# Additions of the drains in the later quarters: VectorE, two per unit over four units, in place of GpSimd, four per unit over two

## The chip, the cores and the metric

The kernel runs on one core of a Trainium2 chip. The metric is the device time of one execution in microseconds. The kernel before took 713.81 us in the median of three runs (713.41 to 713.83). The engines are named as in the profile: PE is TensorE, DVE is VectorE, ACT is ScalarE, POOL is GpSimd, SP is the engine whose queue issues the DMAs.

## The reference

A layer of an FNet block and then a gated feed-forward layer, on x of 2048 rows by 448 columns in float32. Cut to what matters:

```
def _A_ref(x, ...):                          # Fourier mixing, real part only
    a = einsum("bsd,ed->bse", x, dft_hid_re)
    b = einsum("bsd,ed->bse", x, dft_hid_im)
    return einsum("ts,bse->bte", dft_seq_re, a) - einsum("ts,bse->bte", dft_seq_im, b)

def _B_ref(x, w_gate, w_up, w_down):         # 448 -> 1792 -> 448
    g = einsum("bsd,df->bsf", x, w_gate)
    u = einsum("bsd,df->bsf", x, w_up)
    return einsum("bsf,fd->bsd", gelu(g) * u, w_down)

h = x + _A_ref(layernorm(x), ...)
h2 = h + _B_ref(layernorm(h), w_gate, w_up, w_down)
```

The change touches only the very end of the last line: the sum of h and the down projection.

## The kernel before

The Fourier layer fills about the first 346 us. After it the feed-forward layer runs in 42 units, numbered t = 0 to 41, of one gate-and-up step each (`GateUp`): 14 for the first half of the rows, 14 for a third quarter of them, 14 for the fourth. From unit 14 on a unit also carries one or two steps d of the down projection (`COUNT`), 42 in all; the last 14 of 56 steps follow after unit 41.

The matrix products are done by a scheme of seven products in place of eight (Strassen's), and each operand is split into a high and a low half in float16. Every product is made of three matmuls: high by high, high by low and low by high.

**The down projection.** The output is made in eight pieces p = 0 to 7 of 256 rows, here called quarters as the change's title does; seven steps d make one. A step d goes through these stages, each on its engine:

- `hid_load(d)`: SP loads hid[d] (256 KB) from the memory where the gate-and-up units left it.
- `dn_sums(d)`: DVE makes the five sums dn_s of the scheme, three instructions (lines 1174 to 1176).
- `dn_hi(d)`: ACT rounds hid and dn_s to the high halves, in dn_w (line 108).
- `dn_lo(d)`: DVE subtracts these and writes the low halves, in dn_w (line 112). Some steps, done early, write to other places (hops, dn_l, dn_xs).
- `dn_mm(d)`: PE does 21 matmuls into four banks acc_d (line 1212); the third of a step is the first to read a low half.

In unit t the loads and sums are for the steps of unit t + 2, the halves for those of unit t + 1.

**The drain.** When the seven steps of a quarter p are over, at the end of unit t0 (18, 23, 27, 32 and 37 for p = 0 to 4), `Drain` takes the banks to the output piece hr[p], which holds h. ACT copies banks 0 and 1 into v0 and v1 (line 940). DVE adds banks 2 and 3 to hr straight from there (line 944). Then eight additions or subtractions of 128 x 224 in float32, `sums`, bring the four products in v0 and v1 to the four parts of hr (line 972); two read v0, two v1, two v0, two v1. The tiles v0 and v1 exist once: the next quarter's copies must wait for the readers of the last. At last `dn_store(p)` writes hr[p] out (line 1230).

**What sets the order.** It is written out by hand: each engine works through its instructions in the order in which the code issues them, and waits by semaphores for the others. The end of a unit's code is, in this order: the copies and bank additions when a quarter ends, the last gelu (line 1102 on ACT, then a product on POOL, line 1104), the remaining low halves, the sums `dn_sums`, and last the loop over the ended quarters, which the change edits. The next unit's first instruction on DVE is line 1089 (`y3`), which waits for PE; then line 1020 twice (`z2`, `y2`), then the low halves. On SP the next unit's first is `gw_load` (896 KB of weights), which waits for PE, then `hid_load`.

Before the change POOL's eight additions come at the ends of units t0+1 and t0+2, four each, and the store at the end of t0+3.

Of the kernel before, what the change touches and what calls it, by code (L numbers as in the profile page):

```python
# [32 lines left out]
def kernel(  # L33
# [40 lines left out]
    V, A, G, PE = nc.vector, nc.scalar, nc.gpsimd, nc.tensor  # L74
# [242 lines left out]
    class Weights:  # L317
# [8 lines left out]
        def sums(self):  # L326
            gate, up = self.raw[:, 0], self.raw[:, 1]
            s = self.s = prep.tile([P, 10, P], F32, tag="s", name=f"gu_s{self.f}")
            V.tensor_add(s[:, 0:3], up[:, 0:3], up[:, 3:6])
            V.tensor_sub(s[:, 3:6], s[:, 0:3], gate[:, 0:3])  # L330
            V.tensor_sub(s[:, 6:8], gate[:, 0:2], up[:, 0:2])
            V.tensor_sub(s[:, 8:10], gate[:, 4:6], s[:, 4:6])
# [87 lines left out]
    def step_of(n):  # L420

        k, qq = divmod(n - NT, 4)
        return 2 + k // 2, k % 2, qq
# [392 lines left out]
    for n in range(N_STEPS):  # L816
# [78 lines left out]
        else:  # L895
            p, part, qq = step_of(n)
# [29 lines left out]
    class Drain:  # L926
# [27 lines left out]
        def bank3(self):  # L954
            self.add(3, 6, 1.0)

        def sums(self, parts):
            x11, x12, x21, x22 = self.x
            M3, M4, M2, M5 = self.v
            ops = (  # L960
                (G.tensor_add, x12, M3),
                (G.tensor_sub, x21, M4),
                (G.tensor_add, x21, M2),
                (G.tensor_add, x12, M5),
                (G.tensor_sub, x11, M4),
                (G.tensor_add, x22, M3),
                (G.tensor_sub, x11, M5),
                (G.tensor_sub, x22, M2),
            )
            for k in parts:  # L970
                op, x, m = ops[k]
                op(x, x, m)  # L972
# [143 lines left out]
    def gw_load(t):  # L1116
        gw[t] = w_tile(f"gw{t}")
        nc.sync.dma_start(gw[t], w_dram[f_of(t)])
# [4 lines left out]
    def hid_load(d):  # L1123
        p, n = divmod(d, NC)
        hid_in[d] = fpool.tile([P, 4, P], F32, tag="hid", bufs=6, name=f"hid{d}")
        b = max(p // 2 - 1, 0)
        nc.sync.dma_start(hid_in[d], hid_dram[b, n][:, p % 2 if b else p])
# [32 lines left out]
    def dn_sums(d):  # L1160
        t = dn_hid(d)
        if d in LAST:
            spare.append(d)
            s = fops.tile([P, 5, P], F32, tag=("xn", "tt")[len(spare) % 2], name=f"dn_s{d}")
        elif d % 4 < 2:
            if d % 4 == 0:
                opened["l"] = late.tile([P, 10, P], F32, tag="dn_s", name=f"dn_s{d}")
            s = opened["l"][:, d % 4 * 5 :][:, :5]
        else:
            if d % 4 == 2:  # L1170
                opened["s"] = prep.tile([P, 10, P], F32, tag="s", name=f"dn_s{d}")
            s = opened["s"][:, d % 4 % 2 * 5 :][:, :5]
        dn_s[d] = s
        V.tensor_add(s[:, 0:2], t[:, 0:2], t[:, 2:4])  # L1174
        V.tensor_sub(s[:, 2:4], t[:, 1:4:2], t[:, 0:4:2])  # L1175
        V.tensor_add(s[:, 4], t[:, 0], t[:, 3])  # L1176
# [4 lines left out]
    def dn_hi(d):  # L1181
        dn_w[d] = dn_tile(d)
        for src, dst in dn_parts(d):
            hi_part(dn_w[d][:, 0, dst], src)

    def dn_lo(d):
        for src, dst in dn_parts(d):
            lo_part(dn_w[d][:, 1, dst], src, dn_w[d][:, 0, dst])
# [13 lines left out]
    def dn_mm(d, products=range(21)):  # L1202
        p, n = divmod(d, NC)
        if n == 0 and 0 in products:
            dn_banks(p)
        w = dn_w[d]
        for i in products:
            k, m = divmod(i, 3)
            a, b = STRASSEN[k]
            la, lb = ((0, 0), (0, 1), (1, 0))[m]  # L1210
            ps, opens = acc_d[p, "sums"][k]
            PE.matmul(  # L1212
                ps,
                w[:, la, a, :],
                wd[n][:, lb, b, :],
                start=n == 0 and m == 0 and opens,
                stop=n == NC - 1 and m == 2,
                skip_group_check=True,
            )

    def hr_load(p):
        hr[p] = pair_tile(f"hr{p}")
        nc.sync.dma_start(hr[p], h_dram[p])

    def dn_drain(p):
        v = [fpool.tile([P, D], F32, tag=f"v{k}", bufs=1, name=f"v{k}_{p}") for k in range(2)]
        return Drain(hr[p], acc_d.pop(p), v, 1.0 / (H_SC * W_SC))

    def dn_store(p):
        nc.sync.dma_start(outr[p // 4, p % 4], hr[p])  # L1230
# [4 lines left out]
    def do(t, k):  # L1235
        for what in side.pop((t, k), ()):
            what()
# [41 lines left out]
    for t in range(NF):  # L1279
        w = gu.get(t + 2) if t + 2 in JIT_F else None  # L1280
        n = PREP_AT.get(t)
# [89 lines left out]
    drains, ended = {}, {}  # L1371
    for t in range(NF, N_GU):
        now, ahead = steps[t], steps.get(t + 1, [])
        split = EARLY.get(t - 1)
        if t + 2 < N_GU:
            gw_load(t + 2)
        far = steps.get(t + 2, []) + ([EARLY[t + 1]] if t + 1 in EARLY else [])
        far += [47] if t + 1 == N_GU else []
        for d in far + ([52, 53, 54] if t + 1 == N_GU else []):
            hid_load(d)  # L1380
        for d in ahead:
            if d % NC == 0:
                hr_load(d // NC)
        if t in (N_GU - 4, N_GU - 2):
            hr_load(6 + (t == N_GU - 2))
        dn_mm(now[0], range(0, 6))
        prev.y3()
        if t % 2 == 0:
            prev.store()
        cur.y1()  # L1390
        if now[0] % NC:
            cur.z1()
        cur.x2()
        dn_mm(now[0], range(6, 13 if len(now) == 1 else 21))
        for d in ahead:
            dn_hi(d)
        if split is not None:
            dn_hi(split)
        cur.z2()
        do(t, 1)  # L1400
        cur.y2()
        for d in ahead[:1]:
            dn_lo(d)
        if len(now) == 1:
            dn_mm(now[0], range(13, 21))
        else:
            dn_mm(now[1])
        ends = now[-1] % NC == NC - 1
        ends = ends and t + 1 < N_GU
        if ends:  # L1410
            p = now[-1] // NC
            ended[p], drains[p] = t, dn_drain(p)
            drains[p].copy((0,))
        prev = cur
        if t + 1 < N_GU:
            cur = GateUp(t + 1)
            cur.x1()
        if ends:
            drains[p].copy((1,))
            drains[p].bank2()  # L1420
            drains[p].bank3()
            cur.z1()
        prev.c_last()
        for d in ahead[1:]:
            dn_lo(d)
        if split is not None and t + 1 < N_GU:
            dn_lo(split)
        for d in far:
            dn_sums(d)
        do(t, 2)  # L1430
        do(t, 3)
        do(t, 4)
        for p, t0 in ended.items():
            if p < 5 and t - t0 in (1, 2):
                n = 4 * (t - t0)
                drains[p].sums(range(n - 4, n))
            if p < 5 and t - t0 == 3:
                dn_store(p)

    prev.y3()  # L1440
# [99 lines left out]
```

## Time and profile before

| what | value |
|---|---|
| median of three runs | 713.81 us |
| profiled execution, its own time | 712.2 us |
| its span, first to last instruction | 710.2 us |
| PE busy, share of the span | 703.0 us, 99% |
| DVE busy | 531.8 us, 75% |
| ACT busy | 353.2 us, 50% |
| POOL busy | 119.6 us, 17% |
| TensorE clock granted | 1.000 |

A row of the timeline has the start in us from the span's start, the duration, the engine, the line, the operation, output<-inputs, the shape and type, how many were merged, and in brackets how long the engine had been idle and what ended it. A row of groups has the count, then the busy time and the mean in ns of one, then the idle time before them. A row of windows has, after the stretch and its length, the busy time and count on PE, PEld, DVE, ACT and POOL, then the granted clock, the share of the DMA engines and GB/s. A row of waits has who waited for whom, the total, the times and the longest.

### The profile page before, as it was taken

What the parts mean: (1) busy time and instruction counts of PE and PEld (TensorE: products, weight loads), DVE (VectorE), ACT (ScalarE), POOL (GpSimd) and SP (SyncE); (2) the same over time, 40 slices, a digit from 0 to 9 for tenths busy, and PEclk for the clock granted to TensorE, in tenths of its full rate; (3) what the DMA queues carried; (4) which work ended last, traced back from release to release, by engine and by line L of the source; (5) the groups of instructions that cost most, each with busy time, mean ns of one, the idle gap of its engine ahead of it and who ended that gap; (6) DMA issues with size and microseconds to landing.
All of it is one profiled execution on the core that took longest, in us unless ns stands there. A gap on an engine that the chain in (4) does not pass through costs nothing.

```text
span 710.2 us, 13038 instructions
## 1 busy us (share of the span) xinstructions
PE 703.0 (99%) x4952; PEld 480.1 (68%) x4952; DVE 531.8 (75%) x1136; ACT 353.2 (50%) x656; POOL 119.6 (17%) x128
## 2 busy tenths in 40 slices
PE   9999999999999999999999999999999999999998
PEld 5555555555555555797744444469999999989897
DVE  7988637486848779998647787567777866799785
ACT  5776523162526454543436566545555453555531
POOL 0000000000000000000223333311141522352624
PEclk9999999999999999999999999999999999999999
DMA  8788539999898969653755867797797986877512
GB/s 272 244 250 262 124 137 232 238 320 246 207 305 237 269 209 223 257 139 112 173 179 191 280 211 199 199 319 245 192 323 256 258 282 231 295 268 272 206 37 79
DMA packets 116031, 159.42 MB, mean 224 GB/s; under 512 B 61952, under 2 KB 80512, under 8 KB 115968
## 3 DMA queue, kind: packets, MB, share of 16 engines
q1 hardware_dynamic: 115968, 158.60, 73.3%
q8 instruction: 38, 0.62, 0.3%
q14 instruction: 25, 0.20, 0.1%
HBM read 110.33 MB, written 34.34 MB: 204 GB/s over the span
## 4 chain that ended last, share of the span: by engine, by line
PE 95%; DVE 3%; DMA 1%; issue 0%; POOL 0%; SPq 0%; DVEq 0%; POOLq 0%
PE acc L648 33%; PE acc_d L1212 14%; PE pY L1010 14%; PE y L714 9%; PE pZ L1010 9%; PE pX L1010 9%; PE acc_f L520 7%; DMA hid<-hid_dram 1%; DVE dn_s L1175 1%; PE pw L102 1%; DVE dn_s L1174 0%; DVE dn_s L1176 0%; DVE dn_w L112 0%; DVE hops L112 0%; DVE hr L1476 0%
## 5 line engine op out<-in xcount | busy, mean ns | idle before, releaser
L648 PE MATMUL acc<-xs,ws 128*128 128x448 f16 x1248 | 238.0, 352 | 0.0
L648 PEld LDWEIGHTS <-ws 128*128 128x128 f16 x1248 | 122.0, 98 | 114.0 <-DVE ws L114 0.2
L1010 PEld LDWEIGHTS <-gw 128*128 128x128 f16 x1365 | 133.4, 98 | 42.9
L1212 PE MATMUL acc_d<-wd,dn_w 128*128 128x224 f16 x1008 | 111.2, 259 | 2.4 <-DVE dn_w L112 2.4
L1212 PEld LDWEIGHTS <-dn_w 128*128 128x128 f16 x1008 | 96.7, 98 | 5.2 <-DVE dn_w L112 3.2
L1104 POOL TENSOR_TENSOR hs<-hs,c 128x256 f32<-128x256 f32 (+1 forms) x42 | 55.3, 1316 | 225.1 <-ACT c L1102 150.3
L1010 PE MATMUL pY<-hops,gw 128*128 128x256 f16 (+1 forms) x595 | 89.9, 294 | 0.0
L114 DVE SCALAR_TENSOR_TENSOR ws<-wr,ws 128x1024 f16<-128x1024 f32 (+2 forms) x66 | 75.1, 1141 | 8.6 <-ACT ws L108 8.3
L108 ACT ACTIVATE ws<-wr 128x1024 f16<-128x1024 f32 (+2 forms) x66 | 63.8, 981 | 21.5 <-DMA wr<-in_w_seq_dram 20.8
L220 POOL TENSOR_TENSOR wd_s<-wd 128x448 f32<-128x448 f32 x7 | 9.4, 1349 | 342.8 <-DVE r_h L142 342.0
L714 PE MATMUL y<-wh,z 128*128 128x448 f16 x336 | 66.2, 352 | 0.0
L1010 PE MATMUL pX<-hops,gw 128*128 128x256 f16 (+1 forms) x385 | 61.7, 294 | 0.0
L1010 PE MATMUL pZ<-hops,gw 128*128 128x256 f16 (+1 forms) x385 | 61.7, 294 | 0.0
L714 PEld LDWEIGHTS <-z 128*128 128x128 f16 x336 | 32.9, 98 | 30.1
L1020 DVE SCALAR_TENSOR_TENSOR c<-pZ,u 128x256 f32<-128x256 f32 (+1 forms) x42 | 21.4, 510 | 37.8 <-PE pZ L1010 22.3
L520 PEld LDWEIGHTS <-ws 128*128 128x128 f16 x504 | 48.3, 98 | 0.9
L1010 PEld LDWEIGHTS <-gu_w 128*128 128x128 f16 x273 | 26.6, 98 | 31.9 <-issue 0.2
L1055 ACT ACTIVATE pY<-pX 128x256 f32<-128x256 f32 (+1 forms) x42 | 18.4, 439 | 59.3 <-PE pX L1010 58.9
L1066 ACT ACTIVATE u<-pY 128x256 f32<-128x256 f32 (+1 forms) x42 | 19.1, 454 | 55.6 <-PE pY L1010 55.5
L972 POOL TENSOR_TENSOR hr<-hr,v 128x224 f32<-128x224 f32 x56 | 41.8, 772 | 14.7 <-ACT v L940 13.8
L108 ACT ACTIVATE dn_w<-dn_s 128x640 f16<-128x640 f32 x48 | 35.0, 729 | 18.0 <-DVE dn_s L1176 18.0
L112 DVE TENSOR_TENSOR dn_w<-dn_s,dn_w 128x640 f16<-128x640 f32 x48 | 41.6, 867 | 2.0 <-ACT dn_w L108 1.9
(138 smaller groups left out, 880.3 us busy)
## 6 DMA issues: line engine op xcount, KB each, us to landing
gw<-w_dram SPq DMA_DIRECT2D x35, 896.0 KB, 5.4
wr<-in_w_seq_dram SPq DMA_DIRECT2D x100, 256.0 KB, 4.5
hid_dram<-hs SPq DMA_DIRECT2D x27, 512.0 KB, 5.9
hid<-hid_dram SPq DMA_DIRECT2D x54, 256.0 KB, 5.6
w_dram<-gu_w SPq DMA_DIRECT2D x14, 896.0 KB, 5.7
gu_raw<-in_w_gu_dram SPq DMA_DIRECT2D x28, 384.0 KB, 5.9
wr<-in_w_seq_dram SPq DMA_DIRECT2D x14, 512.0 KB, 5.2
x<-in_x_dram SPq DMA_DIRECT2D x16, 224.0 KB, 2.8
```

Source lines behind the costliest of these rows:

```text
L108: A.activation(dst, src, AF.Copy, scale=scale)
L112: V.tensor_sub(dst, src, hi)
L114: V.scalar_tensor_tensor(dst, src, scale, hi, op0=ALU.mult, op1=ALU.subtract)
L520: PE.matmul(fast_sum(n, k), fast_a(n, i, lw, a), fast_b(j, lx, b), start=j == 0 and m == 0 and k % 2 == 0, stop=j == NT // 2 - 1 and m == ...
L648: PE.matmul(acc[key][:, :D], w[:, lw, block * P : (block + 1) * P], xs[c][:, lx, :], start=c == 0 and m == 0, stop=c == NT - 1 and m == 2,)
L714: PE.matmul(y[:, :D], z[p][:, lz, k, g * P : (g + 1) * P], wh[:, lw, k, :], start=k == 0 and m == 0, stop=k == 6 and m == 2,)
L972: op(x, x, m)
L1010: PE.matmul(ps, w[:, wl, wa + ws, :], ops[:, m + ms, :], start=first and n == 0, stop=last and n == len(terms) - 1, skip_group_check=True,)
L1020: V.scalar_tensor_tensor(dst, ps, SC, other, op0=ALU.mult, op1=ALU.add)
L1066: A.activation(self.u2, self.Y, AF.Copy, scale=SC)
L1104: G.tensor_mul(c22, c22, self.cols(self.c12))
L1212: PE.matmul(ps, w[:, la, a, :], wd[n][:, lb, b, :], start=n == 0 and m == 0 and opens, stop=n == NC - 1 and m == 2, skip_group_check=True,)
```

## The change

```diff
-        def sums(self, parts):
+        def sums(self, parts, E=G):
             x11, x12, x21, x22 = self.x
             M3, M4, M2, M5 = self.v
             ops = (
-                (G.tensor_add, x12, M3),
-                (G.tensor_sub, x21, M4),
+                (E.tensor_add, x12, M3),
+                (E.tensor_sub, x21, M4),
...
         for p, t0 in ended.items():
-            if p < 5 and t - t0 in (1, 2):
-                n = 4 * (t - t0)
-                drains[p].sums(range(n - 4, n))
-            if p < 5 and t - t0 == 3:
+            n = 2 * (t - t0)
+            if p < 5 and 2 <= n <= 8:
+                drains[p].sums(range(n - 2, n), V)
+            if p < 5 and n == 8:
                 dn_store(p)
```

The other six operations change G to E in the same way. For the quarters p = 0 to 4 the eight additions go to DVE (`V`), two at the ends of units t0+1 to t0+4; the store goes to the end of t0+4. Quarters 5 and 6, after the units, still call `sums(range(8))` and stay on POOL.

What this makes of the engines' orders is shown at three places. Names carry the number of the step, unit or quarter and then one that a builder gives: dn_s32 is the sum of step 32, hr3 and v1_3 are of quarter 3. A name ending in _49 is a semaphore, by the engine or DMA queue that raises it.

First, DVE at the end of unit 34, the stretch ahead of units 35 and 36. Before:

```order
L1174 TENSOR_TENSOR dn_s32_7237<-hid33_7125 128x256 [waits DMAHW2_49]
L1175 TENSOR_TENSOR dn_s32_7237<-hid33_7125 128x256
L1176 TENSOR_TENSOR dn_s32_7237<-hid33_7125 128x128
L1174 TENSOR_TENSOR dn_s50_7244<-hid50_7127 128x256 [waits DMAHW3_49,DVE_49]
L1175 TENSOR_TENSOR dn_s50_7244<-hid50_7127 128x256
L1176 TENSOR_TENSOR dn_s50_7244<-hid50_7127 128x128
L1089 SCALAR_TENSOR_TENSOR hs_34_7193<-pY_34_7096,g1_34_7164 128x2x128 [waits PE_49]
```

The same place now:

```order
L1174 TENSOR_TENSOR dn_s32_7235<-hid33_7123 128x256 [waits DMAHW2_49]
L1175 TENSOR_TENSOR dn_s32_7235<-hid33_7123 128x256
L1176 TENSOR_TENSOR dn_s32_7235<-hid33_7123 128x128
L1174 TENSOR_TENSOR dn_s50_7242<-hid50_7125 128x256 [waits DMAHW3_49,DVE_49]
L1175 TENSOR_TENSOR dn_s50_7242<-hid50_7125 128x256
L1176 TENSOR_TENSOR dn_s50_7242<-hid50_7125 128x128
L972 TENSOR_TENSOR hr3_6341<-hr3_6341,v1_3_6981 128x224 x2
L1089 SCALAR_TENSOR_TENSOR hs_34_7191<-pY_34_7096,g1_34_7162 128x2x128 [waits PE_49]
```

A pair of additions now stands between the sums and y3; the pair has no wait for another engine.

Second, the boundary of units 27 and 28, where quarter 2 ends only four units after quarter 1. ACT before:

```order
L940 ACTIVATE v0_2_6437<-acc_d2_0_6000 128x448 [waits PE_49,Pool_49]
L1055 ACTIVATE pY_28_6441<-pX_28_6440 128x256 [waits DVE_49,PE_49]
L940 ACTIVATE v1_2_6438<-acc_d2_1_6001 128x448 [waits Pool_49]
L1061 ACTIVATE m5_28_6461<-pZ_28_6454 128x256 [waits PE_49,Activation_49]
L1102 ACTIVATE c12_27_6405<-c12_27_6405 128x256 [waits DVE_49]
```

ACT now:

```order
L940 ACTIVATE v0_2_6434<-acc_d2_0_6000 128x448 [waits DVE_49,PE_49]
L1055 ACTIVATE pY_28_6438<-pX_28_6437 128x256 [waits DVE_49,PE_49]
L940 ACTIVATE v1_2_6435<-acc_d2_1_6001 128x448 [waits DVE_49]
L1061 ACTIVATE m5_28_6458<-pZ_28_6451 128x256 [waits PE_49,Activation_49]
L1102 ACTIVATE c12_27_6402<-c12_27_6402 128x256 [waits Pool_49]
```

And DVE now at the end of unit 27, the rows that the second copy waits for:

```order
L944 SCALAR_TENSOR_TENSOR hr2_5882<-acc_d2_3_6003,hr2_5882 128x224 [waits DVE_49,PE_49]
L1174 TENSOR_TENSOR dn_s22_6462<-hid22_6337 128x256 [waits DMAHW6_49]
L1175 TENSOR_TENSOR dn_s22_6462<-hid22_6337 128x256
L1176 TENSOR_TENSOR dn_s22_6462<-hid22_6337 128x128
L1174 TENSOR_TENSOR dn_s22_6462<-hid23_6339 128x256 [waits DMAHW7_49]
L1175 TENSOR_TENSOR dn_s22_6462<-hid23_6339 128x256
L1176 TENSOR_TENSOR dn_s22_6462<-hid23_6339 128x128
L972 TENSOR_TENSOR hr1_5321<-hr1_5321,v1_1_5958 128x224 x2
L1089 SCALAR_TENSOR_TENSOR hs_26_6284<-pY_27_6316,g1_27_6377 128x2x128 [waits PE_49]
```

The copies waited for POOL, whose additions of quarter 1 stand in units 24 and 25; now they wait for DVE, the first copy for the pair at the end of unit 26, the second for the last pair, which the code issues after the copy in the same unit. By the values of the semaphore it is the second of the two L972 rows above.

Third, SP around the store of quarter 3, before:

```order
L1230 DMA out_0_dram<-hr3_6344 128x2x448 [waits DMAHW0_49,Pool_49]
L1118 DMA gw38_7357<-w_dram5_154 128x3584 [waits DMAHW1_49,PE_49]
L1127 DMA hid35_7359<-hid_dram1_0_3757 128x512 [waits DMAHW2_49,DVE_49]
L1127 DMA hid36_7361<-hid_dram1_1_3758 128x512 [waits DMAHW3_49,DVE_49]
L1127 DMA hid51_7363<-hid_dram2_2_3766 128x512 [waits DVE_49]
L1114 DMA hid_dram2_3_3767<-hs_34_7193 128x1024 [waits DMAHW5_49,DVE_49,Pool_49]
L1118 DMA gw39_7485<-w_dram12_161 128x3584 [waits DMAHW6_49,PE_49]
L1127 DMA hid37_7487<-hid_dram1_2_3759 128x512 [waits DMAHW7_49,DVE_49]
```

And now:

```order
L1118 DMA gw38_7354<-w_dram5_154 128x3584 [waits DMAHW0_49,PE_49]
L1127 DMA hid35_7356<-hid_dram1_0_3757 128x512 [waits DMAHW1_49,DVE_49]
L1127 DMA hid36_7358<-hid_dram1_1_3758 128x512 [waits DMAHW2_49,DVE_49]
L1127 DMA hid51_7360<-hid_dram2_2_3766 128x512 [waits DMAHW3_49,DVE_49]
L1114 DMA hid_dram2_3_3767<-hs_34_7191 128x1024 [waits DVE_49,Pool_49]
L1230 DMA out_0_dram<-hr3_6341 128x2x448 [waits DMAHW5_49,DVE_49]
L1118 DMA gw39_7485<-w_dram12_161 128x3584 [waits DMAHW6_49,PE_49]
L1127 DMA hid37_7487<-hid_dram1_2_3759 128x512 [waits DMAHW7_49,Activation_49]
```

The store stands one unit later and waits for DVE's last pair of that same unit, where it waited for POOL additions of the unit before. The next unit's weights and hid stand behind it.

More of the change, by code (lines that the diff above doesn't have):

```diff
@@ L960, in sums @@
             ops = (
-                (G.tensor_add, x12, M3),
-                (G.tensor_sub, x21, M4),
[L963 to L968, printed above, removed]
+                (E.tensor_add, x12, M3),
+                (E.tensor_sub, x21, M4),
+                (E.tensor_add, x21, M2),
+                (E.tensor_add, x12, M5),
+                (E.tensor_sub, x11, M4),
+                (E.tensor_add, x22, M3),
+                (E.tensor_sub, x11, M5),
+                (E.tensor_sub, x22, M2),
             )
```

## The prediction

> **What bounds the kernel now.** I read the chain of waits first, then the windows for the last two thirds of the program, then what TensorE waits for there, then the timelines around each such wait.
>
> ```profile
> PE 95%; DVE 3%; DMA 1%; issue 0%; POOL 0%; SPq 0%; DVEq 0%; POOLq 0%
> 470.00:678.00 208.00, 205.56 (x1979) 191.44 (x1978) 164.23 (x380) 109.73 (x264) 67.55 (x69) 1.00 0.79 260
> PE acc_d L1212 <- DVE dn_w L112: 2.4, 2, 1.7
> ```
>
> The chain is TensorE for 95%. The change lies in units 19 to 41, which run from about 505 to 678 us, inside the window above: PE busy 205.56 of 208 us, DVE 164.23 (79%), POOL 67.55. The only thing that PE waits for there is dn_w, the low half of the down projection's weights, which VectorE writes. So the change can win no more than these waits, and it can lose whatever it makes VectorE or a bank's release later.
>
> The size of the waits is read from starts, since a PE row's busy time runs past its successor's start:
>
> ```profile
> 574.67 0.74 PE L1212 MATMUL acc_d<-wd,dn_w 128*128 128x224 f16 x6
> 528.08 1.00 PE L1212 MATMUL acc_d<-wd,dn_w 128*128 128x224 f16 x6
> ...
> 630.22 0.35 PE L1212 MATMUL acc_d<-wd,dn_w 128*128 128x224 f16 x2
> 632.24 0.56 PE L1212 MATMUL acc_d<-wd,dn_w 128*128 128x224 f16 x4 [1.67 <-DVE dn_w L112]
> ...
> 669.44 0.35 PE L1212 MATMUL acc_d<-wd,dn_w 128*128 128x224 f16 x2
> 670.49 0.56 PE L1212 MATMUL acc_d<-wd,dn_w 128*128 128x224 f16 x4 [0.69 <-DVE dn_w L112]
> ```
>
> Six such matmuls take 0.74 us when nothing stops them, and two take 0.35, so one starts every (0.74 - 0.35) / 4 = 0.10 us. At 528.08 (unit 22) the six took 1.00: **0.26** lost. At 630.22 (unit 36) the third should start 0.19 after the first, at 630.41; it starts at 632.24: **1.83**. At 669.44 (unit 41) likewise 670.49 - 669.63 = **0.86**. Together 2.95 us.
>
> **What is removed and added.** Four additions at the ends of two units become two at the ends of four, for five quarters: 40 instructions leave POOL and come to DVE. The store of each quarter moves from the end of unit t0+3 to that of t0+4, and the second quarter's last pair now comes after the third quarter's copies.
>
> ```profile
> L972 POOL TENSOR_TENSOR hr<-hr,v 128x224 f32<-128x224 f32 x56 | 41.8, 772 | 14.7 <-ACT v L940 13.8 <-DVE hr L944 0.3
> L582 DVE TENSOR_TENSOR tx<-tx,tx 128x224 f32<-128x224 f32 x8 | 3.1, 393 | 0.8
> ```
>
> POOL gives up 40 x 0.772 = 30.9 us; it is not on the chain, so that alone is worth nothing. DVE's price for the same operation, shape and type is in the trace, on other tiles: 393 ns. So 40 x 0.393 = 15.7 us are added to DVE, 0.79 at the end of a unit. From below it is nothing, where DVE then waits for PE anyway; from above it is the 0.877 that a larger addition took beside POOL (next rows), 1.75 a pair. I take 0.79.
>
> **What POOL's additions cost VectorE today.** Undisturbed, the sums dn_s take this:
>
> ```profile
> L1174 DVE TENSOR_TENSOR dn_s<-hs 128x256 f32<-128x256 f32 x2 | 0.8, 415 | 0.0
> L1176 DVE TENSOR_TENSOR dn_s<-hs 128x128 f32<-128x128 f32 x2 | 0.6, 283 | 0.0
> ```
>
> These two rows are from the tail, where nothing else reads beside them. Now the stretches ahead of each PE wait, grouped, 522.5 to 526.7, 618 to 622.6, 625 to 629.8 and 660 to 667.2:
>
> ```profile
> L1175 DVE TENSOR_TENSOR dn_s<-hid 128x256 f32<-128x256 f32 x2 | 1.8, 914 | 0.0
> L1176 DVE TENSOR_TENSOR dn_s<-hid 128x128 f32<-128x128 f32 x2 | 1.5, 747 | 0.0
> L1174 DVE TENSOR_TENSOR dn_s<-hid 128x256 f32<-128x256 f32 x2 | 1.3, 652 | 1.2 <-DMA hid<-hid_dram 1.2
> ...
> L1175 DVE TENSOR_TENSOR dn_s<-hid 128x256 f32<-128x256 f32 x2 | 1.8, 877 | 0.0
> L1176 DVE TENSOR_TENSOR dn_s<-hid 128x128 f32<-128x128 f32 x2 | 1.5, 744 | 0.0
> L112 DVE TENSOR_TENSOR hops<-dn_s,hops 128x640 f16<-128x640 f32 x1 | 0.8, 810 | 0.0
> ...
> L1174 DVE TENSOR_TENSOR dn_s<-hid 128x256 f32<-128x256 f32 x2 | 1.8, 880 | 0.0
> L112 DVE TENSOR_TENSOR hops<-dn_s,hops 128x640 f16<-128x640 f32 x1 | 1.3, 1345 | 0.0
> L1175 DVE TENSOR_TENSOR dn_s<-hid 128x256 f32<-128x256 f32 x2 | 1.3, 643 | 0.0
> L1176 DVE TENSOR_TENSOR dn_s<-hid 128x128 f32<-128x128 f32 x2 | 1.0, 510 | 0.0
> ...
> L112 DVE TENSOR_TENSOR dn_w<-dn_s,dn_w 128x640 f16<-128x640 f32 x2 | 2.2, 1076 | 0.0
> L112 DVE TENSOR_TENSOR dn_w<-hid,dn_w 128x256 f16<-128x256 f32 x2 | 1.3, 640 | 0.0
> L112 DVE TENSOR_TENSOR dn_l<-dn_s,dn_l 128x640 f16<-128x640 f32 x1 | 1.3, 1276 | 0.0
> L112 DVE TENSOR_TENSOR dn_l<-hid,dn_l 128x256 f16<-128x256 f32 x1 | 0.9, 875 | 0.0
> ```
>
> And what POOL did in the last two of them:
>
> ```profile
> 625.65 3.50 POOL L972 TENSOR_TENSOR hr<-hr,v 128x224 f32<-128x224 f32 x4
> ...
> 662.84 4.03 POOL L972 TENSOR_TENSOR hr<-hr,v 128x224 f32<-128x224 f32 x4
> ```
>
> Additions of 0.415 take 0.88 exactly while the four L972 run. Excess over 0.415, 0.283 and 0.810: first stretch 2 x 0.499 + 2 x 0.464 + 2 x 0.237 = **2.40**; second 2 x 0.462 + 2 x 0.461 = 1.85; third 2 x 0.465 + 0.535 + 2 x 0.228 + 2 x 0.227 = 2.38; second and third together **4.23**; fourth 2 x 0.266 + 2 x 0.225 + 0.466 + 0.460 = **1.91**, without its dn_s. DVE has no idle time in the last three (0.0 in each row), so all of it arrives at dn_w.
>
> The SBUF page of the Trainium skill (SBUF — State Buffer, Who interferes with whom) says that a VectorE instruction with two SBUF inputs contends with a GpSimd one that reads SBUF, and that the later one blocks until the other ends. The rows above agree: 0.88 beside L972 against 0.415 alone.
>
> **The sum.** Unit 22: 2.40 won, one pair (0.79) in the way, the pair before it falls into the 1.2 us for which DVE waits for a DMA; 1.6 is more than 0.26, so the wait goes. Unit 36: 4.23 - 2 x 0.79 = 2.65, more than 1.83: gone. Unit 41: 1.91 - 0.79 = 1.12, more than 0.86: gone. What is late next there is PE itself, with 0.3 us and more to spare. That is **-2.95**.
>
> **The new wait.** At the end of unit 27 the order shows ScalarE's copy of bank 1 of the third quarter into v1 waiting for VectorE's last pair of the second quarter, which stands behind both dn_s of the unit; before, it waited for POOL additions long done.
>
> ```profile
> 574.50 0.54 ACT L940 ACTIVATE v<-acc_d 128x448 f32<-128x448 f32 x1
> ...
> 574.80 0.42 DVE L1174 TENSOR_TENSOR dn_s<-hid 128x256 f32<-128x256 f32 x1
> 575.67 0.42 DVE L1174 TENSOR_TENSOR dn_s<-hid 128x256 f32<-128x256 f32 x1
> 577.08 0.41 DVE L1089 SCALAR_TENSOR_TENSOR hs<-pY,g 128x256 f32<-128x256 f32 x1
> ...
> 575.70 0.98 POOL L1104 TENSOR_TENSOR hs<-hs,c 128x256 f32<-128x256 f32 x1 [8.06 <-ACT c L1102]
> 576.99 0.83 PE L1212 MATMUL acc_d<-wd,dn_w 128*128 128x224 f16 x7
> ```
>
> One dn_s takes 0.87 (574.80 to 575.67). The second took 1.41 beside POOL's L1104, whose gelu input ScalarE computes behind the copy; it therefore moves away, and the second takes 0.87 too: free at 576.54, the pair done at 577.33. The copy (0.54) ends at 577.87 in place of 575.04, and PE, which opens that bank at 576.99, starts it about 0.1 later than that: **+1.0**. If L1104 still gets in the way it is +1.5. Behind the copy on ScalarE stand m, c, u, g and the high halves of unit 29, 0.4 us each; PE moves 1.0 itself and then has 7 matmuls before it needs m, so no second wait follows. From below: nothing, if VectorE has caught up more than I think; but it waits for PE in unit 27, so it has not.
>
> Elsewhere the pairs fall where DVE then waits for z2 of its unit. The tail after 678 us is untouched. Sum: -2.95 + 1.0 = **-1.95** us: the profiled execution's 712.2 (span 710.2 and 2.0 around it) to 710.25. The median shown is 1.6 above that execution; the difference is put on it: 713.81 - 1.95 = **711.9**.
>
> **Rivals.** (1) *The store stands in front of loads.* It now waits on SP's queue for the unit's last pair, ahead of the next unit's weights and hid:
>
> ```profile
> 604.85 1.42 SPq L1127 DMA_DIRECT2D hid<-hid_dram  x3
> hid<-hid_dram SPq DMA_DIRECT2D x54, 256.0 KB, 5.6
> ...
> 611.16 0.92 DVE L1174 TENSOR_TENSOR dn_s<-hid 128x256 f32<-128x256 f32 x1
> 615.28 0.41 DVE L112 TENSOR_TENSOR dn_w<-hid,dn_w 128x256 f16<-128x256 f32 x1
> 615.66 0.74 PE L1212 MATMUL acc_d<-wd,dn_w 128*128 128x224 f16 x6
> ```
>
> Of the four places (units 23, 28, 33, 37) this has the least room: dn_w ends at 615.69, PE needs it 0.19 after 615.66, 0.16 to spare. The load would be issued some 0.8 later, at 605.6, and land at 611.2, just in time; with 0.459 MB of store (128 x 896 x 4 bytes) in front at the window's 260 GB/s it lands 1.8 later and PE loses 1.65. Then -1.95 + 1.65 = -0.3: 713.5. For it: DMA is busy 0.79 in the window. [...]
>
> (2) *VectorE becomes the bound (slower).* If the slow rows are DVE's own, or if the added pairs block against L1104 as they did against L972, nothing is won, and the pairs add to each wait: unit 22 0.79, unit 36 2 x 0.79, unit 41 0.79, and the copy's 1.0: +4.2, 718.0. It decides as soon as the relief in a stretch is under 0.79 a pair. Against: the slow rows end with the L972 rows. The Trainium skill's Perfetto Trace Analysis (Optimizing Scalar/DVE Operations) speaks for it: a saturated DVE is to be relieved, even to GpSimd; this change does the reverse. It adds that moving work between those two may not help, since they share a port, which would be no change.
>
> (3) *The new wait is covered* by ScalarE and PE running otherwise there: -2.95, 710.9.
>
> (4) *The waits of this execution are its own.* They rest on landings, 1.2 us in unit 22; if in the timed runs they are half, -1.5 + 1.0 = -0.5: 713.3.
>
> **How the numbers follow.** Forecast 0.52; (1) 0.18; (2) 0.08; (3) 0.10; (4) 0.12. About 0.2% (1.4 us) is what a measurement of this kernel can tell from no change. The forecast with its copy at +1.5 is -1.45, on that border, so some of its weight counts as same. Faster 0.57, same 0.33, slower 0.10. Range: (3) below, (1) and (4) above, 710.7 to 713.8, leaving out (2) and the ends.
>
> **What would show it.** Right: the page has 16 L972 on POOL and 40 on DVE at about 0.39; dn_s means near 0.42; the waits at units 22, 36 and 41 gone; one new PE wait of about 1 us for ScalarE's v at the start of unit 28. Wrong: dn_s still near 0.88 somewhere; DVE's dn_w still ending PE waits; dn_s waiting longer for hid in units 28, 33 and 37.

## The result and the profile after

The changed kernel took 711.44 us in the median of eight runs (710.24 to 712.03), beside 713.43 for the kernel before (712.44 to 714.91, eight runs): a ratio of 0.9971, 95% interval 0.9960 to 0.9982. That is 2.0 us faster; the prediction had 1.95 (its 711.9 lies 0.5 above the median, mostly because it starts from the 713.81 of three runs). The profiled execution took 711.16 with a span of 708.7, 1.5 less than the span before.

The page, first part, then the heads of the chain of waits:

```profile
PE 702.7 (99%) x4952; PEld 480.3 (68%) x4952; DVE 531.7 (75%) x1176; ACT 353.3 (50%) x656; POOL 92.6 (13%) x88
...
PE 97%; DMA 1%; DVE 1%; SPq 0%; ACT 0%; issue 0%; POOL 0%; DVEq 0%; POOLq 0%; ACTq 0%
```

VectorE has 40 instructions more and is busy as long as before, 531.7 against 531.8. DVE's share of the chain fell from 3% to 1%. Where the time of the 40 came from shows in the groups of the whole span (count, then busy, mean ns, then idle before):

```profile
L1174 DVE TENSOR_TENSOR dn_s<-hid 128x256 f32<-128x256 f32 x54 | 25.4, 471 | 15.7 <-DMA hid<-hid_dram 15.6
L1175 DVE TENSOR_TENSOR dn_s<-hid 128x256 f32<-128x256 f32 x54 | 24.5, 454 | 0.0
...
L1176 DVE TENSOR_TENSOR dn_s<-hid 128x128 f32<-128x128 f32 x54 | 16.7, 310 | 0.0
...
L972 DVE TENSOR_TENSOR hr<-hr,v 128x224 f32<-128x224 f32 x40 | 14.2, 394 | 0.0
...
L972 POOL TENSOR_TENSOR hr<-hr,v 128x224 f32<-128x224 f32 x16 | 11.0, 715 | 14.3 <-ACT v L940 13.8 <-DVE hr L944 0.3
```

Before, the three rows of sums were 28.7 (531 ns), 28.6 (530 ns) and 19.9 (369 ns): 10.6 us have gone there, near the 14.2 that came. VectorE's wait for hid grew, 11.7 to 15.6.

PE's waits, from 470 to 680 us; then its six matmuls ahead of the weights at the places where the prediction read its three losses (units 22, 36 and 41):

```profile
PE acc_d L1212 <- ACT v L940: 0.7, 1, 0.7
PE acc_d L1212 <- DVE dn_w L112: 0.5, 1, 0.5
```

```profile
528.72 0.74 PE L1212 MATMUL acc_d<-wd,dn_w 128*128 128x224 f16 x6
...
631.46 0.74 PE L1212 MATMUL acc_d<-wd,dn_w 128*128 128x224 f16 x6
...
668.84 0.74 PE L1212 MATMUL acc_d<-wd,dn_w 128*128 128x224 f16 x6
```

All three run their six in 0.74: the three waits are gone. The wait of 0.5 for dn_w that is left ends at 478.97, in unit 15, ahead of the first instruction that the change moves (unit 19); by starts it cost 0.69. It goes back to a store: VectorE could not write the tile hs again until the store of its last content (hid_dram<-hs) had landed, which took 8.3 us from its issue, where it took 7.3 before. These are VectorE's rows there, before and after; its low half for PE comes right behind:

```profile
477.37 0.42 DVE L1020 SCALAR_TENSOR_TENSOR hs<-pY,m 128x256 f32<-128x256 f32 x1 [0.49 <-DMA hid_dram<-hs]
```

```profile
478.16 0.42 DVE L1020 SCALAR_TENSOR_TENSOR hs<-pY,m 128x256 f32<-128x256 f32 x1 [1.35 <-DMA hid_dram<-hs]
```

The other wait is the new one, at the start of unit 28:

```profile
576.82 0.71 PE L1010 MATMUL pX<-hops,gw 128*128 128x256 f16 x5
578.24 0.83 PE L1212 MATMUL acc_d<-wd,dn_w 128*128 128x224 f16 x7 [0.71 <-ACT v L940]
578.90 0.71 PE L1010 MATMUL pZ<-hops,gw 128*128 128x256 f16 x5
579.45 0.82 PE L1010 MATMUL pY<-hops,gw 128*128 128x256 f16 x6
...
577.64 0.54 ACT L940 ACTIVATE v<-acc_d 128x448 f32<-128x448 f32 x1 [2.68 <-DVE hr L972]
...
575.18 0.42 DVE L1174 TENSOR_TENSOR dn_s<-hid 128x256 f32<-128x256 f32 x1
...
576.05 0.42 DVE L1174 TENSOR_TENSOR dn_s<-hid 128x256 f32<-128x256 f32 x1
...
576.92 0.69 DVE L972 TENSOR_TENSOR hr<-hr,v 128x224 f32<-128x224 f32 x2
577.52 0.42 DVE L1089 SCALAR_TENSOR_TENSOR hs<-pY,g 128x256 f32<-128x256 f32 x1
```

ScalarE stood idle 2.68 us until VectorE's last pair of quarter 1 let its copy start, and PE stood for the copy. Five such matmuls take 0.55 to the next start, as the five of pZ show (578.90 to 579.45); so L1212 should start at 577.37 and starts at 578.24: 0.87 lost. Over units 19 to 41 that makes -2.95 + 0.87 = -2.08, with +0.69 of unit 15 beside it: the 1.4 that PE's starts show between the two traces there, of the 1.5 of the spans. The 0.69 belongs to this execution, since the code up to unit 19 is the same.

### The profile page after: what moved, and what is told of

The parts are those of the page before. It is cut to its first block, busy times and chain, and to the rows that moved or that the text cites. A ratio compares the mean times of both kernels' runs of the same rounds, so it can differ in the third digit from the quotient of the medians.

```text
span 708.7 us, 13039 instructions
## 1 busy us (share of the span) xinstructions
PE 702.7 (99%) x4952; PEld 480.3 (68%) x4952; DVE 531.7 (75%) x1176; ACT 353.3 (50%) x656; POOL 92.6 (13%) x88
## 4 chain that ended last, share of the span: by engine, by line
PE 97%; DMA 1%; DVE 1%; SPq 0%; ACT 0%; issue 0%; POOL 0%; DVEq 0%; POOLq 0%; ACTq 0%
PE acc L648 33%; PE acc_d L1212 15%; PE pY L1010 14%; PE pZ L1010 9%; PE y L714 9%; PE pX L1010 9%; PE acc_f L520 7%; DMA hid_dram<-hs 1%; PE pw L102 1%; DVE hr L1476 0%; DVE hr L944 0%; DVE dn_s L1175 0%; DVE dn_s L1174 0%; DVE hr L972 0%; ACT u L1066 0%
## 5 line engine op out<-in xcount | busy, mean ns | idle before, releaser
L1212 PE MATMUL acc_d<-wd,dn_w 128*128 128x224 f16 x1008 | 110.8, 259 | 1.2 <-ACT v L940 0.7
L1212 PEld LDWEIGHTS <-dn_w 128*128 128x128 f16 x1008 | 96.8, 98 | 3.6 <-issue 0.9
L1104 POOL TENSOR_TENSOR hs<-hs,c 128x256 f32<-128x256 f32 (+1 forms) x42 | 58.7, 1398 | 251.1 <-ACT c L1102 183.9
L1174 DVE TENSOR_TENSOR dn_s<-hid 128x256 f32<-128x256 f32 x54 | 25.4, 471 | 15.7 <-DMA hid<-hid_dram 15.6
```

What stands on the lines that cost most here:

```text
L1104: G.tensor_mul(c22, c22, self.cols(self.c12))
L1212: PE.matmul(ps, w[:, la, a, :], wd[n][:, lb, b, :], start=n == 0 and m == 0 and opens, stop=n == NC - 1 and m == 2, skip_group_check=True,)
```

## Experiments

The change has three parts: the engine, the pace, and the place of the store, which follows the pace. In the table, each ratio is to the kernel before on the same chip (713.1 to 713.6 in these sessions); "PE idle" is 208.00 less the busy time of PE in the window 470 to 678 us of the profiled execution.

| kernel | median us | ratio, 95% interval | PE idle |
|---|---|---|---|
| before | 713.43 | 1 | 2.44 |
| the change | 711.44 | 0.9971, 0.9960 to 0.9982 | 1.23 |
| 1 quarters 0, 3, 4 alone | 711.23 | 0.9979, 0.9969 to 0.9988 | 0.97 |
| 2 quarters 1, 2 alone | 714.02 | 1.0006, 0.9994 to 1.0019 | 3.55 |
| 3 VectorE, four per unit | 710.75 | 0.9968, 0.9957 to 0.9980 | 0.49 |
| 4 change, two buffers of v1 | 710.31 | 0.9962, 0.9950 to 0.9975 | 0.55 |
| 5 no additions | 709.95 | 0.9956, 0.9943 to 0.9970 | 0.00 |
| 6 three instructions for one | 730.41 | 1.0251, 1.0232 to 1.0269 | (other stages) |
| 7 GpSimd, two per unit | 714.14 | 1.0013, 1.0004 to 1.0023 | 2.06 |
| 8 as 4, store behind the loads | 710.06 | 0.9960, 0.9947 to 0.9974 | 0.00 |
| 9 as 7, store behind the loads | 710.01 | 0.9954, 0.9941 to 0.9966 | 0.21 |
| 10 change, store behind the loads | 710.79 | 0.9963, 0.9951 to 0.9976 | 0.71 |
| 11 one input in place of two | 709.60 | 0.9947, 0.9932 to 0.9962 | 0.00 |
| 12 before, store as in 9 | 713.61 | 1.0005, 0.9996 to 1.0014 | 2.88 |

Rows of that view for five of them, in the order change, 8, 9, 10 and 12 (after the stretch and its length: busy time and count on PE, PEld, DVE, ACT, POOL; clock, DMA share, GB/s):

```profile
470.00:678.00 208.00, 206.77 (x1994) 192.94 (x1993) 165.02 (x423) 110.88 (x266) 40.57 (x29) 1.00 0.79 258
```

```profile
470.00:678.00 208.00, 208.00 (x2002) 193.93 (x2000) 165.88 (x425) 110.89 (x267) 39.29 (x29) 1.00 0.80 260
```

```profile
470.00:678.00 208.00, 207.79 (x2006) 194.03 (x2004) 162.85 (x386) 110.69 (x266) 66.73 (x69) 1.00 0.79 259
```

```profile
470.00:678.00 208.00, 207.29 (x2000) 193.60 (x1999) 164.49 (x423) 110.50 (x266) 41.38 (x29) 1.00 0.80 259
```

```profile
470.00:678.00 208.00, 205.12 (x1966) 189.80 (x1965) 164.17 (x378) 109.92 (x264) 65.69 (x68) 1.00 0.80 257
```

### 1 and 2: the gain and the price, by quarters

The loop of the change gets a branch with the pace and engine of before, for quarters 1 and 2 in experiment 1, and for (0, 3, 4) in experiment 2:

```diff
         for p, t0 in ended.items():
+            if p in (1, 2):
+                if t - t0 in (1, 2):
+                    n = 4 * (t - t0)
+                    drains[p].sums(range(n - 4, n))
+                if t - t0 == 3:
+                    dn_store(p)
+                continue
```

> Quarters 0, 3 and 4 as in the change, quarters 1 and 2 as before. Theory (relief from POOL's additions in three stretches, price at the boundary of units 27 and 28): all of the gain and none of the loss, 713.4 - 2.95 = 710.5; the PE waits for dn_w at units 22, 36 and 41 are gone and the PE wait for v1 at unit 28 too. Rival (the gain comes from all quarters alike): three fifths of the measured 2.0, 712.2. Rival (VectorE's load is the price everywhere): nearer 711.4, as after.

> The other half: quarters 1 and 2 as in the change, 0, 3 and 4 as before. Theory: none of the gain, the three dn_w waits stay at about 2.95 in all, and the new wait for v1 is added, 713.4 + 0.9 = 714.3. Rival (the gain comes from all quarters alike): two fifths of 2.0 won, 712.6.

Experiment 2 keeps the losses at units 22, 36 and 41 and gets the one at unit 28:

```profile
579.61 0.83 PE L1212 MATMUL acc_d<-wd,dn_w 128*128 128x224 f16 x7 [0.70 <-ACT v L940]
...
633.29 0.35 PE L1212 MATMUL acc_d<-wd,dn_w 128*128 128x224 f16 x2
635.34 0.56 PE L1212 MATMUL acc_d<-wd,dn_w 128*128 128x224 f16 x4 [1.70 <-DVE dn_w L112]
```

By starts the four are 0.51 (unit 22), 0.87 (28), 1.87 (36) and 0.86 (41), and two of 0.2 stand beside them. The time, 714.02, lies where the theory put it, though its interval takes in no change; the rival's 712.6 lies just below the interval (713.25 x 0.9994 = 712.82). Its twelve runs spread from 711.51 to 715.40, and the profiled one is the longest of them, so its waits may be longer than in most. In experiment 1 none of these four is there. It was expected at 710.5 and took 711.23: a part of the gain was lost in another way. Its trace has one wait, at unit 26, of 1.14 by starts, where VectorE stood 3.43 us for a hid load that took 8.45 us to land and then made the sums beside quarter 1's four additions on GpSimd. Whether that wait is in most of its runs stays open; by time alone the rival's 712.2 isn't excluded.

### 3: the engine without the pace

The edit is against the kernel before; `sums` is the change's, which takes the engine as an argument:

```diff
             if p < 5 and t - t0 in (1, 2):
                 n = 4 * (t - t0)
-                drains[p].sums(range(n - 4, n))
+                drains[p].sums(range(n - 4, n), V)
             if p < 5 and t - t0 == 3:
                 dn_store(p)
```

> The additions on VectorE, but four per unit over two units and the store at t0+3, the pace of before: the engine alone is changed. Theory: relief as in the change, and quarter 1 is done two units before quarter 2's copies, so no wait for v1: 713.4 - 2.95 = 710.5. Rival (spreading is what keeps VectorE's load bearable): four additions take 1.57 at one place, and of the stretch ahead of unit 36, four and four stand in it with a relief of 4.23, which is 1.09 won against a wait of 1.83: a wait of 0.74 stays there, 711.3 or more.

710.75. The copy into v1 waits for nothing, units 22 and 41 have no wait, and from unit 19 to 41 one alone is over 0.11: at unit 36, 0.65 stays by starts, near the rival's 0.74:

```profile
629.21 1.29 DVE L972 TENSOR_TENSOR hr<-hr,v 128x224 f32<-128x224 f32 x4
630.42 0.42 DVE L1089 SCALAR_TENSOR_TENSOR hs<-pY,g 128x256 f32<-128x256 f32 x1
```

The four end just ahead of the chain of y3, z2, y2 and dn_w that PE waits for there, and take 1.21 of it. So the engine alone wins most, and in the trace spreading is worth the rest. The time can't tell the theory's 710.5 from the rival's 711.3: the interval takes in both (710.2 to 711.8).

### 4: the new wait removed

```diff
-        v = [fpool.tile([P, D], F32, tag=f"v{k}", bufs=1, name=...
+        v = [fpool.tile([P, D], F32, tag=f"v{k}", bufs=1 + k, name=...
```

> The change, with two buffers for v1, so that quarter 2's copy need not wait for quarter 1's last pair. Theory: the PE loss of 0.87 at the start of unit 28 goes and nothing comes in its place: 711.4 - 0.9 = 710.6. Rival (something else is late there at once, such as the bank additions or ScalarE's m): 711.4, and another releaser stands at PE's start at unit 28.

710.31: the theory's 710.6 fits, and the rival's 711.4 is at the edge of the interval (713.25 x 0.9975 = 711.47). PE's row at unit 28 has no wait, and no other stands in its place. What is left in units 19 to 41 is 0.27 at unit 34, where hid had landed late behind the store.

### 5 and 6: what the additions may cost at most, and what they cost three times over

Experiment 5 leaves the loop's call of `sums` out, and with it the additions of quarters 0 to 4. Experiment 6 repeats each:

```diff
                 op(x, x, m)
+                if E is V:
+                    back = V.tensor_sub if op == V.tensor_add else V.tensor_add
+                    back(x, x, m)
+                    op(x, x, m)
```

> Leaves out the additions of quarters 0 to 4 on every engine (the store at t0+3 stays). Theory (a change here can win no more than the PE waits): 713.4 - 2.95 = 710.5, no lower than the change with two buffers of v1, and no PE wait for dn_w beyond what late hid loads make. Rival (the 15.7 us of additions on VectorE still cost time in the change): lower than the change with two buffers of v1 by over 0.7.

> The change with each addition on VectorE followed by its opposite and by itself again: six instructions at the end of a unit in place of two, 2.36 us in place of 0.79. Theory (a pair stands in front of dn_w in full, and the change's slacks at units 22, 34, 36 and 41 were 0.5, 0.1, 0.4 and 0.9): +1.0, +1.4, +2.8 and +0.7 there and +1.6 at the copy into v1, 711.4 + 7 = about 718. Rival (pairs fall where VectorE waits for PE anyway, so that only the copy feels them): 711.4 + 1.6 = 713.0.

Without additions there is no wait for PE at all from 470 to 678, and the time is 709.95. That is the floor for any place of these additions; it is 1.5 below the change, and not measurably below experiments 4, 8 and 9. So the 14.2 us of additions on VectorE cost nothing by themselves.

Three times over they cost 19.0, far more than either expectation. PE's waits from 470 to 690 us (its lines are shifted by four), and the chain of the page:

```profile
PE acc_d L1216 <- DVE dn_w L112: 11.9, 9, 2.2
PE acc_d L1216 <- ACT v L940: 2.4, 1, 2.4
PE pZ L1014 <- DVE c L1024: 0.5, 1, 0.5
```

```profile
PE 85%; DVE 8%; DMA 5%; issue 1%; ACT 0%; SPq 0%; POOL 0%; DVEq 0%; POOLq 0%
```

About 3.4 of the 19.0 are not waits: PE's clock stood at half twice for 3.41 us each (last section), which leaves 15.6. The 80 extra instructions, at the 1.21 / 4 = 0.30 that one takes from start to start in experiment 3, are 24 us; so VectorE could hide about 8 of them. I had priced four places for dn_w with the slack that they had in the change; there are nine. I read this as one unit's loss that the next can't make up, which was not tested apart. So VectorE becomes the bound somewhere between the change's load and three times its additions; no run lies between.

### 7, 9 and 12: the pace without the engine

In experiment 7 the change's loop calls `sums` without V. Quarter 1 keeps four per unit over two: with two per unit, ScalarE's copy into v1 would wait for a pair on POOL that stands behind the product L1104, which waits for a gelu that stands behind that copy.

```diff
             n = 2 * (t - t0)
-            if p < 5 and 2 <= n <= 8:
-                drains[p].sums(range(n - 2, n), V)
+            if p != 1 and p < 5 and 2 <= n <= 8:
+                drains[p].sums(range(n - 2, n))
+            if p == 1 and t - t0 in (1, 2):
+                drains[p].sums(range(2 * n - 4, 2 * n))
```

> The additions stay on GpSimd but at the change's pace, two per unit over four units, and the store where the change has it (quarter 1 alone keeps four per unit over two). Theory (VectorE's loss lies in POOL's reading, wherever it is spread): dn_s beside L972 still takes about 0.88, the sums of L1174 and L1175 keep a mean near 530 ns, the wait at unit 36 is made smaller, not removed, as a part of the additions comes behind it: 712.5 to 713.4. Rival (the pace is what helps): the waits for dn_w go and the time is near 710.5.

It took 714.14, more than the kernel before. But its waits don't stand where they did: units 22, 36 and 41 have none, and there is one of 1.50 by starts at unit 34, with 0.76 near unit 39 and 0.28 near unit 26. These make 2.54, less than the 2.95 before, so why its median is above that of before stays open. The SP rows at that quarter's store, experiment 7 and then 9 (next):

```profile
607.33 0.39 SPq L1230 DMA_DIRECT2D out_dram<-hr  x1
607.81 0.42 SPq L1118 DMA_DIRECT2D gw<-w_dram  x1
608.33 1.88 SPq L1127 DMA_DIRECT2D hid<-hid_dram  x3
```

```profile
604.62 0.32 SPq L1118 DMA_DIRECT2D gw<-w_dram  x1
605.03 1.50 SPq L1127 DMA_DIRECT2D hid<-hid_dram  x3
606.58 0.47 SPq L1230 DMA_DIRECT2D out_dram<-hr  x1
```

In 7 the store waits on SP for the pair on POOL, and the loads of hid are issued 3.3 us later than in 9, of which 1.1 are the execution's own (POOL's L1104 just ahead stands at 605.35 against 604.27). VectorE then stood 1.76 us for them, and PE 1.34:

```profile
614.25 0.43 DVE L1174 TENSOR_TENSOR dn_s<-hid 128x256 f32<-128x256 f32 x1 [1.76 <-DMA hid<-hid_dram]
...
618.61 0.56 PE L1212 MATMUL acc_d<-wd,dn_w 128*128 128x224 f16 x4 [1.34 <-DVE dn_w L112]
```

So 7 mixed two causes. Experiment 9 takes the store out of the way, and 12 is its control, the kernel before with the store in that same place:

```diff
         for d in far + ([52, 53, 54] if t + 1 == N_GU else []):
             hid_load(d)
+        if late_store:
+            dn_store(late_store.pop())
...
             if p < 5 and n == 8:
-                dn_store(p)
+                late_store.append(p)
```

> The additions on GpSimd at two per unit as in the kernel before this, and the store issued behind the next unit's weights and hid loads. That kernel's PE waits stood where the store had held up the loads (unit 34: 1.50, near unit 39: 0.76), not at units 22, 36 and 41. Theory A (the reading beside VectorE is the cost, spreading it alone wins little): dn_s stays slow beside L972 and waits of 1 to 2 us come back near units 36 and 41, 712.5 or more. Theory B (spreading is enough on either engine, and the store was what spoiled it): no PE wait over 0.3 in units 19 to 41, 713.2 - 2.7 = 710.5.

> The kernel before, GpSimd with four per unit over two units, and only the store moved to where the kernel with two per unit on GpSimd and the late store has it, so that those two differ in the pace alone. Theory B (the pace is what wins there): waits of about 3 us in all stay at units 22, 36 and 41, and the time is that of before, 713.1. Rival (the store's place gave that kernel its gain): near 710.0.

710.01 and 713.61: the two differ in the pace alone, and each is set beside the kernel before on its own chip. The pace with the store moved wins 3.1 us (0.9954), the store moved alone wins nothing (1.0005), and the intervals are apart; every addition is still on GpSimd. Theory B holds. Experiment 12 keeps the wait at unit 36 as it was:

```profile
631.35 0.35 PE L1212 MATMUL acc_d<-wd,dn_w 128*128 128x224 f16 x2
633.39 0.56 PE L1212 MATMUL acc_d<-wd,dn_w 128*128 128x224 f16 x4 [1.69 <-DVE dn_w L112]
```

POOL's rows ahead of that place show what the pace does, together with one row of VectorE's low halves. First before; behind these came four more L972 at 625.65 (3.50):

```profile
619.12 3.44 POOL L972 TENSOR_TENSOR hr<-hr,v 128x224 f32<-128x224 f32 x4
624.91 0.78 POOL L1104 TENSOR_TENSOR hs<-hs,c 128x256 f32<-128x256 f32 x1 [2.35 <-ACT c L1102]
625.03 1.34 DVE L112 TENSOR_TENSOR hops<-dn_s,hops 128x640 f16<-128x640 f32 x1
```

And in 9:

```profile
616.81 2.52 POOL L1104 TENSOR_TENSOR hs<-hs,c 128x256 f32<-128x256 f32 x1 [4.83 <-ACT c L1102]
619.30 1.27 POOL L972 TENSOR_TENSOR hr<-hr,v 128x224 f32<-128x224 f32 x2
625.09 3.51 POOL L1104 TENSOR_TENSOR hs<-hs,c 128x256 f32<-128x256 f32 x1 [4.53 <-ACT c L1102]
628.57 1.27 POOL L972 TENSOR_TENSOR hr<-hr,v 128x224 f32<-128x224 f32 x2
```

The first pair is over after 1.27, and VectorE comes to its next instructions earlier: it begins the low half of that row at 624.59, ahead of L1104 (625.09), where before it came 0.12 behind it. Now it is POOL that is held: L1104 takes 3.51 where it took 0.78, the low half takes 0.81 where it took 1.34, and the additions of all three steps' sums (L1174, L1175) run at 0.41. The later pair falls beside y3 and z2, which stay at 0.41 and 0.42. The means over the whole stretch fall little (500 to 678 us: L1174 from 534 to 518 ns, L1175 from 546 to 504); it is the sums ahead of the critical place that are spared.

### 8 and 10: the store out of the way in the change

The same edit of the store, on experiment 4 (8) and on the change (10).

> The change with two buffers of v1, and the store issued behind the next unit's weights and hid loads on SP in place of ahead of them. Theory: the load of hid is issued as early as before in units 23, 28, 33 and 37, VectorE's wait of 2.3 to 3.8 for it in unit 28 is near 0.3, and the 0.27 that PE lost at unit 34 with two buffers of v1 goes: 710.3 - 0.3 = 710.0. Rival (the loads land as late for other reasons): 710.3 and the same 0.27 at unit 34.

> The change, with one buffer of v1 as it has, and the store behind the next unit's weights and hid loads. Theory (the store's delay was not on PE's path in the change, the copy into v1 was): PE loses about 0.9 at unit 28 and nothing else after unit 19, 711.4 - 0.1 = 711.3. Rival (the store's delay is what the change pays in most runs): nearer 710.1, as with two buffers of v1.

Experiment 8 has no PE wait left from 470 to 678 and takes 710.06, as the theory had it. Experiment 10 has the 0.87 at unit 28 alone, as expected, but took 710.79, between the two expectations; against the change (711.44, another session) the intervals overlap, so whether the store costs the change some tenths in its common run is not settled. In the profiled execution it cost PE nothing.

### 11: what GpSimd reads

```diff
             for k in parts:
                 op, x, m = ops[k]
-                op(x, x, m)
+                if m is not None:
+                    G.tensor_scalar(x, x, 1.0, None, op0=ALU.mult)
```

> The kernel before with each of GpSimd's additions, in all quarters, replaced by a product of hr with 1.0 in place: one input in place of two, v0 and v1 are not read and their additions left out. Theory (GpSimd's reading as such slows VectorE): dn_s beside L972 stays near 0.88, the waits at units 22, 36 and 41 stay, and the time is within 0.5 of 713.2. Rival (only GpSimd instructions with two inputs do it): dn_s at 0.41 beside L972, no such wait, 713.2 - 2.9 = 710.3.

709.60, and no PE wait. The instruction takes GpSimd about as long as the addition did, 809 ns in the mean. Lines are shifted by one here:

```profile
619.68 3.26 POOL L973 TENSOR_SCALAR hr<-hr 128x224 f32<-128x224 f32 x4
620.62 0.61 DVE L1175 TENSOR_TENSOR dn_s<-hid 128x256 f32<-128x256 f32 x1
```

Beside these four in a row (619.68 to 622.94) the additions of the sums took 0.41 to 0.61, where beside four additions most took 0.88. Neither end was right about the duration: this instruction slows VectorE too, but by up to a half, not to twice, and that is not enough to be seen by PE. It differs from the addition in its kind as well as in its number of inputs; which of the two matters was not tested.

## Why the prediction was right, point by point

- **The bound and the three waits** (-2.95): right. PE's waits at units 22, 36 and 41 are gone in the change, and experiment 5 shows that nothing more than PE's waits could be had.
- **POOL's additions slow VectorE's sums**: right, but narrower than it was put. The rows of sums gave back 10.6 us. But not every row beside L972 was slow (at 620.83 one L1174 took 0.41 among the four L972), and in each of the sums for units 22, 36 and 41 the prediction counted a slow row of VectorE's that stood beside L1104, which stays on POOL: 0.95 at 522.91, 1.34 at 625.03 and 1.34 at 662.22, 0.53 too long each. Without it the relief is 1.87, 3.70 and 1.38; less the pairs of 0.79 that is enough for units 22 and 36, and 0.59 for the 0.86 at unit 41. In the change this share stays at units 22 and 41 (0.95 at 523.57 and at 661.89). The wait at unit 41 went all the same: two rows of sums that the prediction left out there (0.87 and 0.88 at 665.48 and 666.28) fell to 0.41 as well, 0.92 in all. So unit 41 was right in part by luck. The SBUF page of the Trainium skill (SBUF — State Buffer, Who interferes with whom) has a sentence that I had not weighed, "Issue order, not op shape, decides who blocks"; the trace agrees as far as it goes: L1104 took 0.78 where it came ahead of VectorE's low half (624.91 and 625.03) and 3.51 where it came behind it (625.09 and 624.59), and then it was held through a whole series of VectorE's instructions, not through one.
- **What wins**: this is the step that was incomplete. I treated the change as a change of engine and had no rival for its pace. The pace alone wins all (9 against 12), as long as the store does not stand ahead of the loads (in 7, where it does, nothing is won); the engine alone wins most (3); together (8) they are not measurably worth more than the pace.
- **The price of a pair** (0.79 for two of 393 ns): too high. Durations overlap at VectorE; from start to start the pair takes 577.52 - 576.92 = 0.60. By this alone the margins at units 22, 36 and 41 were larger by 0.2 to 0.4 than computed.
- **The new wait** (+1.0): right, 0.87, at the copy and behind the pair named; experiment 2 shows it without the gain, and 4 the gain without it. Rival 3 (that it would be covered) falls.
- **Rival 1, the store ahead of the loads**: its mechanism is real. In the change the load of unit 28 was issued at 578.63, behind the store, where it had been 576.40 (0.4 of it is the execution's own), and VectorE stood 2.31 for it; PE did not feel it there. In experiment 4 PE lost 0.27 to it at unit 34, the place that the prediction named as the tightest, and 1.50 in 7.
- **Rival 2, VectorE as the bound**: not at this load, but the point from which it decides is near: 24 us of further additions cost 19.0, about 3.4 of it by PE's clock.
- **Rival 4, waits of one execution**: falls. The same waits were in the traces of experiments 2 and 12 (1.87 and 1.86 at unit 36), and the timed runs show the gain.

The best kernels are 8 and 9, both near 710.0, at the floor of experiment 5. Number 9 moves no work to VectorE: two additions per unit on GpSimd, quarter 1 as before, the store behind the loads.

## What to carry to other kernels

When an engine that is far from full slows a busy one, ask first whether its work comes in a burst at one place; the same work at half the pace on the same engine may be as good as moving it, as it was here, so try the pace apart from the engine. Whatever is done later keeps its buffer longer and carries its store along: look who writes that buffer next, and what stands behind the store on its queue. And price a short instruction in a row by its distance from start to start, not by its duration: the pair took 0.60 here, where two durations make 0.79.

## What the hardware showed that I had not expected

In experiment 6, PE's granted clock fell to half twice, from 645.07 to 648.49 and from 679.21 to 682.62 us: 3.41 us each, and the starts lie ten times 3.41 apart. Cut into steps of 3.41 on that grid, the rows of its windows show what came before (PE stands first behind the length, the clock behind POOL). First the two steps of one case, then those around the longest wait:

```profile
641.66:645.07 3.41, 1.26 (x13) 1.04 (x12) 3.34 (x8) 0.69 (x2) 0.72 (x1) 1.00 0.02 7
645.07:648.49 3.42, 3.42 (x18) 2.37 (x17) 3.42 (x10) 0.77 (x2) 0.00 (x0) 0.50 0.71 218
```

```profile
580.22:583.63 3.41, 2.21 (x21) 1.86 (x20) 3.31 (x11) 0.00 (x0) 0.00 (x0) 1.00 0.03 11
583.63:587.05 3.42, 2.22 (x22) 2.10 (x22) 1.45 (x5) 2.82 (x9) 0.73 (x1) 1.00 0.59 168
```

A wait of 2.15 us that lay within one step was followed by a step at 0.50, and so was one of 1.99 (676.5 to 678.5). The longest wait, 2.40, was cut in two by an edge of the grid (1.20 in each step), and the clock stayed at 1.00; in no other step from 470 to 700 us did PE stand over 1.4. The Trainium skill (TensorE: Matmul & The Clock Gate, Part 1) has the half rate after an idle window of about 3.4 us; no wait here was that long. Here 2.0 us of idle time in one step of 3.41 was enough; that the grid decides is read from these two cases in one trace and was not tested. So such a wait at PE can cost about 1.7 us more than itself (half of 3.41).

And the slowing goes both ways: POOL's product L1104 takes 0.72 alone and up to 5.03 us (before, at 632.36) beside VectorE's sums and low halves. It is not on PE's path here.
